# Turning x and the result by block transposes on VectorE and 128-byte DMA pieces, in place of transposes on TensorE

## The chip, the cores and the metric

The kernel runs on one core of a Trainium2 chip (trn2). The metric is device time in microseconds for one launch; three runs were timed. One further execution was profiled. The core has five engines that matter here: TensorE (PE, with its weight loads shown as PEld), VectorE (DVE), ScalarE (ACT), GpSimd (POOL) and SyncE (SP). DMAs are issued by the queues of SP and ACT ("SPq" and "ACTq" in the profile).

## The reference

An attention with RMS-normalised q and k is followed by an MLP mixer. Sizes: batch B = 8, 12 heads of 64, 448 tokens, so 768 channels; the token MLP has 256 hidden units, the channel MLP 1536. All inputs are float32 but the four mixer weights, which are float64.

```python
q_n, k_n = rmsnorm(q, g_q), rmsnorm(k, g_k)
attn = softmax(q_n @ k_n.T / 8)                       # per batch and head
x = (attn @ v).transpose(0, 2, 1, 3).reshape(8, 448, 768)
h = np.maximum(x.transpose(0, 2, 1) @ w_tok1, 0) @ w_tok2   # over tokens
u = x + h.transpose(0, 2, 1)
h2 = np.maximum(u @ w_ch1, 0) @ w_ch2                 # over channels
return u + h2
```

## The kernel before

The work of one batch lives in a tile `uT` of [128 channels, 6 groups of channels, 448 tokens]. Attention writes x into it, transposed: each pair of heads gives one group `j` (the normalisation by the row sums, `denominator`, is the last step and ends on VectorE at L468). So everything has channels on partitions, except for two places:

- the token MLP's first product, `tok1` (L598), needs x with tokens on partitions. `trans_x` makes it, one group of channels at a time, into the tile `x` of [112, 4, 384], one for each half of the channels;
- the result must be written to DRAM with tokens as rows. `trans_y` does that, one group at a time, through a tile `y`.

Both call `turn`: four transposes on TensorE (L577) from `uT` into a PSUM tile of the pool that the attention's scores also use (`ps_S`, 4 buffers), and a copy from PSUM on ACT (L581) or on DVE (L583). `trans_y` then issues one DMA on ACT's queue (L822). There are 48 turns of x and 48 of the result.

The 448 tokens are taken as 112 partitions by 4: partition p holds tokens 4p to 4p + 3, in q's load (`load_qk`, L1006), in the load of `w_tok1` and `w_tok2` (`weight_chunks`), in `x` and in the output DMA. So inside the kernel the tokens are permuted, and put right by the output DMA.

The order of the work on PE, DVE, ACT and POOL is written out by hand; the queue of SP is ordered by the program builder. Work is put into lists of items (a cost in us and a function), and `merge` interleaves the lists evenly by cost. While batch b goes through the mixer, batch b + 1 goes through the attention. One pass of the loop over b does this:

1. `tok1` on half 0 of x, merged with the last two turns of the result of b - 1 (`left`);
2. the attention of the next batch merged with `tok1` on half 1, `tok2` (L606, whose result DVE adds to `uT` at L611), the first channel product `ch1` (L728) and the two-column part of the second, `ch2` (L785);
3. `last_items`: the seven one-column products of `ch2`, in which four turns of this batch's result and six turns of the next batch's x are interleaved.

`tok1` and the products of `ch1`, `ch2` and `tok2` use a PSUM pool `ps_M` of two buffers. The result of `tok1` passes through a ReLU on ACT (L601) into `h1`. The weights of the channel MLP come as "units" through six SBUF buffers by DMAs on SP's queue (L654, `load_units`), five units ahead of their use. In the first batches SP also carries the load, conversion and storage of the weights and of their sums.

```python
l = turns(b, [0, 1, KC, KC + 1])
if b + 1 < B:
    l += x_items(b + 1, 0) + x_items(b + 1, 1)
return [single[0]] + merge(single[1:-1], l) + [single[-1]]
```

The program holds two arms of the whole kernel, chosen by a test on g_q and g_k at run time; the inputs take the first one (`shifted` is False), and all of the profile is of that.

Of the kernel before, what the change touches and what calls it, by code (L numbers as in the profile page):

```python
# [8 lines left out]
F32 = mybir.dt.float32  # L9
# [7 lines left out]
DRAM = bass.MemoryType.DRAM  # L17
# [9 lines left out]
def merge(*lists):  # L27

    totals = [sum(c for c, _ in l) or 1.0 for l in lists]
    done = [0.0] * len(lists)  # L30
    at = [0] * len(lists)
    res = []
    while True:
        live = [i for i in range(len(lists)) if at[i] < len(lists[i])]
        if not live:
            return res
        i = min(live, key=lambda i: (done[i] + lists[i][at[i]][0] / 2) / totals[i])
        c, fn = lists[i][at[i]]
        at[i] += 1
        done[i] += c  # L40
        res.append((c, fn))
# [3 lines left out]
def whole(ctx, tc, shifted, pre, q, k, v, g_q, g_k, moe_w_tok1, moe_w_tok2, moe_w_ch1, moe_w_ch2, out):  # L45


    nc = tc.nc
# [3 lines left out]
    B, H, S, D = q.shape  # L52
# [3 lines left out]
    P = 128  # L56
    NS = 4
    R = S // NS
# [3 lines left out]
    NC = C // P  # L62
    NF = DC // P
    HC = C // 2
    HN = NS // 2
    HS = S // 2
    KC, KF = NC // 2, NF // 2
# [8 lines left out]
    pool = lambda name, bufs, **kw: ctx.enter_context(tc.tile_pool(name=name, bufs=bufs, **kw))  # L76
# [8 lines left out]
    rd_pool = pool("rd_pool", 2)  # L85
    uT_pool = pool("uT_pool", 2)
    x_pool = pool("x_pool", 2)
    y_pool = pool("y_pool", 3)
    h1_pool = pool("h1_pool", 2)
    tu_pool = pool("tu_pool", 1)  # L90
    r_pool = pool("r_pool", 1)
    stage_pool = pool("stage_pool", 3)
    unit_pool = pool("unit_pool", UNITS)
    dram = pool("dram", 1, space=DRAM)
    ps_S = pool("ps_S", 4, space=PSUM)
    ps_O = pool("ps_O", 2, space=PSUM)
    ps_M = pool("ps_M", 2, space=PSUM)

    ident, one_c, expo_c, g_t = pre.ident, pre.one_c, pre.expo_c, pre.g_t
    w1_sb = const.tile([P, NS, DT], F32, name="w1_sb")  # L100
    w2_sb = const.tile([P, NJ, NS, R], F32, name="w2_sb")
# [12 lines left out]
    WCOLS = 512  # L114

    def weight_chunks():

        first, second = [], []
        w1v = moe_w_tok1.rearrange("(p c) n -> p c n", c=NS)
        for c in range(0, NS, 2):  # L120
            first.append((R, [w1v[:, c:c + 2, :].rearrange("p c n -> p (c n)")], w1_sb[0:R, c:c + 2, :].rearrange("p c n -> p (c n)"), None))
        for j in range(NJ):
            dst = w2_sb[:, j].rearrange("p c r -> p r c")
            first.append((P, [moe_w_tok2[j * P:(j + 1) * P, :]], dst, NS))

        for w, group, m, t in stages:
            rows = (DC if w is moe_w_ch2 else C) // 2
            src = [w[r:r + P].rearrange("p (i n) -> p i n", i=2)[:, :, m * P:(m + 1) * P]
                   for r in (t * P, rows + t * P)]
            second.append((P, src, None, None))  # L130
        return first, second

    def stage_list():
# [4 lines left out]
        return l  # L138

    def columns(i):  # L140
        return WCOLS if chunks[i][2] is None else chunks[i][1][0].shape[-1]

    def raw_tile():
        return raw_pool.tile([P, WCOLS, 2], U32, name="raw")

    def weight_load(i):
        rows, srcs, dst, split = chunks[i]
        n = columns(i) // len(srcs)
        wide = srcs[0].dtype == I64
        t = raw_tile()  # L150
        if not wide:
            t = t[:].rearrange("p n w -> p (n w)").bitcast(F32)
        for k, src in enumerate(srcs):
            to = t[0:rows, k * n:(k + 1) * n]
            if wide:
                src = src.bitcast(U32)
                to = to.rearrange("p (i n) w -> p i (n w)", i=2) if dst is None else to.rearrange("p n w -> p (n w)")
            elif dst is None:
                to = to.rearrange("p (i n) -> p i n", i=2)
            nc.sync.dma_start(out=to, in_=src)  # L160
        st["raw", i] = t

# [68 lines left out]
            out=hi, in0=hi, scalar=0x80000000, in1=e, op0=ALU.bitwise_and, op1=ALU.bitwise_or)  # L231

    def convert_last(i):
        rows, srcs, dst, split = chunks[i]
        n = columns(i)
        if dst is None:
            q = st["stage", i - len(first)] = stage_pool.tile([P, 4, P], F32, name="stage")
            dst = q[:].rearrange("p q n -> p (q n)")
        fold = (lambda a: a.rearrange("p (r c) -> p r c", c=split)) if split else (lambda a: a)
        t = st.pop(("raw", i))  # L240
        if srcs[0].dtype != I64:
            nc.gpsimd.tensor_copy(out=dst, in_=fold(t[0:rows, 0:n]))
        else:
            lo, hi = (fold(t[0:rows, 0:n, w].bitcast(F32)) for w in range(2))
            nc.gpsimd.tensor_tensor(out=dst, in0=lo, in1=hi, op=ALU.mult)  # L245
    def weight_items(lo, hi):

# [322 lines left out]

    def turn(b, j, dst, by_act):

        ps = s_tile("t_ps")
        for c in range(NS):
            nc.tensor.transpose(  # L577
                ps[0:R, c * P:(c + 1) * P], st["uT", b][:, j, c * R:(c + 1) * R], ident[:, :])
        src = ps[0:R, :].rearrange("p (c n) -> p c n", c=NS)
        if by_act:  # L580
            nc.scalar.copy(out=dst, in_=src)  # L581
        else:
            nc.vector.tensor_copy(out=dst, in_=src)  # L583

    def trans_x(b, j):

        half, o = divmod(j * P, HC)
        if o == 0:
            st["x", half] = x_pool.tile([P, NS, HC], F32, name="x")
        turn(b, j, st["x", half][0:R, :, o:o + P], j % 2)  # L590

    def tok1(b, jc, h):
        cs = slice(h * HC, (h + 1) * HC)
# [223 lines left out]
            into(nc.vector, 1, 0, got)  # L817

    def trans_y(b, cc):
        y = y_pool.tile([P, NS, P], F32, name="y")  # L820
        turn(b, cc, y[0:R], True)
        nc.scalar.dma_start(  # L822
            out=out[b].rearrange("(p c) n -> p c n", c=NS)[:, :, cc * P:(cc + 1) * P], in_=y[0:R])

    turns = lambda b, cs: [(0.5, lambda cc=cc: trans_y(b, cc)) for cc in cs]
    us = lambda n, cols: n * cols * 4 / 2400

    def x_items(b, h):
        return [(0.5, lambda j=j: trans_x(b, j)) for j in range(h * NC // 2, (h + 1) * NC // 2)]

    def tok1_items(b, h):
        return [(us(NS, HC), lambda j=j, h=h: tok1(b, j, h)) for j in range(NJ)]
# [16 lines left out]
    def last_items(b, sums):  # L849


        single = [(us(6, HS), lambda i=i: ch2(b, 1, i, 0)) for i in range(7)]
        if b == 0:
            single = merge(
                [(us(6, S), lambda o=o, h=h: ch2_first(o, h, 2)) for o in range(2) for h in range(2)], sums)
        l = turns(b, [0, 1, KC, KC + 1])
        if b + 1 < B:
            l += x_items(b + 1, 0) + x_items(b + 1, 1)
        return [single[0]] + merge(single[1:-1], l) + [single[-1]]


# [36 lines left out]
    per = NPAIR * 2  # L898
    att_items = lambda lo, hi: [it for g in range(lo, hi) for it in att_step(g)]
# [5 lines left out]
    for b in range(B):  # L905
        early, double = middle_items(b)
        if b == 0:
            begin = x_items(0, 1) + tok1_items(0, 0) + tok1_items(0, 1)
            early = merge(begin + early, weight_items(BEFORE, then)) + merge(
                double, weight_items(then, len(chunks) + 3) + sums[:6])  # L910
        else:

            for _, fn in merge(tok1_items(b, 0), left):
                fn()
            if b == 1:
                early, double = merge(early, sums[12:33]), merge(double, sums[33:])
            early = tok1_items(b, 1) + early + double
        lo = (b + AHEAD) * per + 1
        att = att_items(lo, lo + per) if b + AHEAD < B else []
        for _, fn in merge(att, early) + last_items(b, sums[6:12]):  # L920
            fn()
        left = turns(b, [2, KC + 2])
# [4 lines left out]
class Start:  # L927
# [66 lines left out]
    def load_qk(self, p, st, other=None):  # L994


        b, hs = self.heads(p)
        D, NS, P = self.D, self.NS, 128
        if ("qk", p) not in st:
            st["qk", p] = self.qk_t[p % 3]  # L1000
        qk = st["qk", p]
        nk = (NS - 1) * P
        q = qk[0:self.R, 0:2 * NS * D].rearrange("p (c h d) -> p c h d", c=NS, h=2)
        k = qk[:, 2 * NS * D:4 * NS * D - 2 * D].rearrange("p (c h d) -> p c h d", c=NS - 1, h=2)
        for a in range(2):
            self.nc.sync.dma_start(out=q[:, :, a], in_=self.q[b, hs][a].rearrange("(p c) d -> p c d", c=NS))  # L1006
        for a in range(2):
            (other or self.nc.sync).dma_start(
                out=k[:, :, a], in_=self.k[b, hs][a][0:nk].rearrange("(p c) d -> p c d", c=NS - 1))
        for a in range(2):  # L1010
            o = 4 * NS * D - 2 * D + a * D
            self.nc.sync.dma_start(out=qk[a * D:(a + 1) * D, o:o + D], in_=self.k[b, hs][a][nk:])
# [124 lines left out]
```

## Time and profile before

| | |
|---|---|
| median of 3 runs | 1450.26 us (1448.8 to 1451.36) |
| the profiled execution | 1450.25 us; span of its instructions 1448.5 us |
| PE busy | 97% of the span |
| DVE, ACT, POOL busy | 47%, 33%, 29% |
| clock granted to TensorE | 0.989 of full speed |
| mean DMA rate | 152 GB/s, 256811 packets, 108004 of them under 512 bytes |
| PE transposes of L577 | 384 |

The busy shares are averages over the span. A row of the profile names the line of the kernel, the engine, the operation and "out<-in" by the tiles' names; where an engine sat idle, the row ends with the idle time and with what ended it, after an arrow. A DMA has two times: how long its issue held the queue, and how long after the start of the issue its data had landed. A product in float32 appears as two matmul records, so that 6 matmuls are "x12".

### The profile page before, as it was taken

The numbers are of one execution on the slowest core, as the hardware profiler recorded it, in microseconds if no ns is written. First come the engines' busy times: TensorE is split into PE (matmuls) and PEld (weight loads), VectorE is DVE, ScalarE is ACT, GpSimd is POOL, SyncE is SP. The second block draws the span as 40 slices with busy tenths as digits, with TensorE's granted clock in tenths as the row PEclk, the third lists the DMA queues.
The fourth block names the chain that finished last, engine by engine and source line by source line (L and its number), as shares of the span: only waits on it lengthen the run. The fifth ranks groups of instructions, "written<-read, shape, count | busy, mean of one in ns | idle before, by whom it ended". The sixth has DMA issues, their size and how long they took to land.

```text
span 1448.5 us, 19051 instructions
## 1 busy us (share of the span) xinstructions
PE 1398.2 (97%) x6832; PEld 992.3 (69%) x6832; DVE 681.5 (47%) x1270; ACT 471.5 (33%) x845; POOL 423.3 (29%) x425
## 2 busy tenths in 40 slices
PE   5888989999999999999999999999999999999998
PEld 2333434456778677785787767785877847777997
DVE  7878887316543444425543255334454244332311
ACT  5644445223332233223332233323332233212111
POOL 1122323417763123312332033321233123311230
PEclk9988999999999999999999999999999999999999
DMA  6556768565986245452545434452454514334453
GB/s 175 167 154 196 217 184 237 158 188 162 269 255 209 76 128 149 137 167 65 154 128 150 132 101 144 142 172 69 135 145 144 161 46 142 124 114 132 142 174 117
DMA packets 256811, 219.47 MB, mean 152 GB/s; under 512 B 108004, under 2 KB 215524, under 8 KB 256708
## 3 DMA queue, kind: packets, MB, share of 16 engines
q1 hardware_dynamic: 233506, 206.96, 48.3%
q10 hardware_dynamic: 23074, 11.21, 3.0%
q8 instruction: 56, 0.92, 0.3%
q14 instruction: 47, 0.39, 0.1%
q0 software_dynamic: 128, 0.00, 0.0%
HBM read 188.22 MB, written 29.88 MB: 151 GB/s over the span
## 4 chain that ended last, share of the span: by engine, by line
PE 88%; DVE 6%; issue 2%; SPq 1%; DMA 1%; ACT 1%; POOL 0%; ACTq 0%; DVEq 0%; POOLq 0%
PE m_ps L728 24%; PE m_ps L785 23%; PE s_ps L320 8%; PE o_ps L421 8%; PE m_ps L598 5%; PE m_ps L606 4%; PE m_ps L709 4%; PE m_ps L691 3%; PE t_ps L577 3%; PE t_ps L300 2%; PE d_ps L400 2%; PE o_ps L433 1%; PE s_ps L334 1%; DVE raw L211 1%; DVE raw L230 1%
## 5 line engine op out<-in xcount | busy, mean ns | idle before, releaser
L785 PE MATMUL m_ps<-hb,unit 128*128 128x224 f32 x1764 | 349.7, 354 | 0.1
L785 PEld LDWEIGHTS m_ps<-hb,unit 128*128 128x128 f32 x1764 | 327.8, 190 | 17.0 <-issue 12.1
L310 ACT ACTIVATE e<-s_ps,rs 128x448 f32<-128x448 f32 x336 | 187.4, 634 | 209.0 <-PE s_ps L320 133.8
L728 PE MATMUL m_ps<-tu,unit 128*128 128x224 f32 x1008 | 204.5, 354 | 0.0
L728 PEld LDWEIGHTS m_ps<-tu,unit 128*128 128x128 f32 x1008 | 187.5, 190 | 9.2 <-PE o_ps L421 4.2
L728 PE MATMUL m_ps<-uT,unit 128*128 128x224 f32 x756 | 153.8, 356 | 1.8 <-DVE uT L611 1.8
L728 PEld LDWEIGHTS m_ps<-uT,unit 128*128 128x128 f32 x756 | 141.0, 190 | 19.8 <-issue 16.4
L320 PE MATMUL s_ps<-qkT 64*128 64x448 f32 x576 | 142.5, 589 | 5.3 <-ACT qkT L302 2.8
L421 PE MATMUL o_ps<-e,v 128*64 128x448 f32 x576 | 133.2, 566 | 0.0
L794 POOL TENSOR_TENSOR uT<-uT,r 128x448 f32<-128x448 f32 (+1 forms) x56 | 50.0, 903 | 224.7 <-DVE r L794 144.0
L381 POOL TENSOR_TENSOR es<-e 128x896 f32<-128x896 f32 x42 | 89.8, 2138 | 71.0 <-ACT sq L1029 51.4
L290 POOL TENSOR_TENSOR qk_t<-qk_t,rs 112x512 f32<-112x512 f32 x36 | 39.3, 1113 | 239.9 <-DVE rs L1067 200.6
L320 PEld LDWEIGHTS s_ps<-qkT 64*128 64x128 f32 x576 | 51.5, 192 | 72.4 <-issue 55.8
L462 DVE STREAM_TRANSPOSE dt<-d_ps 128x448 f32<-128x448 f32 x42 | 27.3, 650 | 153.2 <-PE d_ps L400 153.1
L302 ACT ACTIVATE qkT<-t_ps,g_t 128x448 f32<-128x448 f32 (+1 forms) x96 | 60.3, 660 | 118.8 <-PE t_ps L300 117.6
L421 PEld LDWEIGHTS o_ps<-e,v 128*64 128x64 f32 x576 | 33.2, 137 | 86.8 <-issue 82.3
L794 DVE TENSOR_TENSOR uT<-uT,m_ps 128x448 f32<-128x448 f32 (+1 forms) x70 | 34.1, 502 | 117.3 <-PE m_ps L785 117.1
L733 DVE TENSOR_TENSOR r<-m_ps,r 128x448 f32<-128x448 f32 x63 | 39.2, 622 | 106.3 <-POOL r L733 63.2
L606 PE MATMUL m_ps<-w_sb,h 128*128 128x448 f32 x192 | 80.8, 564 | 8.6 <-DVE uT L611 8.5
L598 PE MATMUL m_ps<-x,w_sb 112*128 112x384 f32 x256 | 88.1, 489 | 0.0
L387 DVE TENSOR_TENSOR es<-es,e 128x896 f32<-128x896 f32 x42 | 46.3, 1103 | 87.8 <-ACT e L310 63.8
L245 POOL TENSOR_TENSOR stage<-raw 128x512 f32<-128x512 f32 x36 | 41.5, 1154 | 143.5 <-DVE raw L230 66.4
(93 smaller groups left out, 1584.5 us busy)
## 6 DMA issues: line engine op xcount, KB each, us to landing
unit<-ws SPq DMA_DIRECT2D x318, 384.0 KB, 3.3
raw<-in_moe_w_ch_dram SPq DMA_DIRECT2D x72, 256.0 KB, 3.4
out_dram<-y ACTq DMA_DIRECT2D x48, 224.0 KB, 3.3
qk_t<-in_q_dram SPq DMA_DIRECT2D x84, 112.0 KB, 3.5
v<-in_v_dram SPq DMA_DIRECT2D x48, 192.0 KB, 2.7
ws<-stage SPq DMA_DIRECT2D x36, 256.0 KB, 3.8
raw<-ws SPq DMA_DIRECT2D x36, 256.0 KB, 3.8
ws<-raw SPq DMA_DIRECT2D x36, 256.0 KB, 3.6
```

The source lines that it names most:

```text
L302: nc.scalar.mul(to, ps[:, 0:NS * n], g_t[:, i:i + 1])
L310: nc.scalar.activation(out=out, in_=ps[:, 0:S], func=AF.Exp, scale=st["rs", p][:, r:r + 1])
L320: nc.tensor.matmul(out=pss[a][:, 0:S], lhsT=qkT[a * D:(a + 1) * D, o:o + P], rhs=qkT[a * D:(a + 1) * D, 0:S], start=True, stop=True)
L381: nc.gpsimd.tensor_tensor(out=es[:], in0=st["e", p, 0][:], in1=st["e", p, 1][:], op=ALU.add)
L387: nc.vector.tensor_tensor(out=es[:], in0=es[:], in1=st["e", p, 2][:], op=ALU.add)
L421: nc.tensor.matmul(out=o[a * D:(a + 1) * D, 0:S], lhsT=vt[:, c:c + D], rhs=e[:, a, :], start=start, stop=stop)
L598: nc.tensor.matmul(out=ps[:, 0:HC], lhsT=w1_sb[0:R, c, jc * P:(jc + 1) * P], rhs=st["x", h][0:R, c, :], start=(c == 0), stop=(c == NS - 1))
L606: nc.tensor.matmul(out=ps[:, 0:S], lhsT=st["h1", jc][:, cc * P:(cc + 1) * P], rhs=w2_sb[:, jc].rearrange("p c r -> p (c r)"), start=(jc == ...
L709: nc.tensor.matmul(out=ps[:, 0:S], lhsT=w, rhs=natural(half)[:, :, t, :], start=(half == 0 and t == 0), stop=(half == 1 and t == KF - 1))
L728: nc.tensor.matmul(out=ps[:, j * HS:(j + 1) * HS], lhsT=w[:, t, j, :], rhs=m, start=(t == 0), stop=(t == KC - 1))
L785: nc.tensor.matmul(out=ps[:, j * HS:(j + 1) * HS], lhsT=st["w"](j, t), rhs=hb[:, HB[what], t, :], start=(t == 0), stop=(t == KF - 1))
L794: add = lambda e, o, x, y: e.tensor_tensor(out=o, in0=x, in1=y, op=ALU.add)
```

## The change

`turn` no longer uses TensorE, PSUM or a copy. VectorE transposes the 32x32 blocks of one group of `uT` (128 channels by 448 tokens) in one instruction, from SBUF to SBUF, into a tile of a new pool with four buffers. Four DMAs, one for each block row of 32 channels, then put the pieces at their places in DRAM: 32 x 14 pieces of 32 floats (128 bytes) each. For the result they go straight to the output, issued by ACT. For x they go into a DRAM tile `xs` of [448, 384], issued by SP, and when three groups are done one DMA on SP reads the half of x back into `x` with tokens on partitions.

The tokens are in natural order: token c x 112 + p lies on partition p, chunk c. So the loads of q and of `w_tok1` have another pattern, and `w_tok2` is taken without a fold of its columns.

The order changes too: half 0 of the next batch's x is turned in the middle of the attention, after its eighth step, and half 1 at the head of the list in `last_items`, ahead of the result's turns. The cost of a turn in the lists is 0.1 in place of 0.5.

```diff
-    y_pool = pool("y_pool", 3)
+    turn_pool = pool("turn_pool", 4)
...
+    xs_pool = pool("xs_pool", 2, space=DRAM)
...
-        w1v = moe_w_tok1.rearrange("(p c) n -> p c n", c=NS)
+        w1v = moe_w_tok1.rearrange("(c p) n -> p c n", c=NS)
...
-            dst = w2_sb[:, j].rearrange("p c r -> p r c")
-            first.append((P, [moe_w_tok2[j * P:(j + 1) * P, :]], dst, NS))
+            first.append((P, [moe_w_tok2[j * P:(j + 1) * P, :]], w2_sb[:, j].rearrange("p c r -> p (c r)")))
...
-    def turn(b, j, dst, by_act):
-
-        ps = s_tile("t_ps")
-        for c in range(NS):
-            nc.tensor.transpose(
-                ps[0:R, c * P:(c + 1) * P], st["uT", b][:, j, c * R:(c + 1) * R], ident[:, :])
-        src = ps[0:R, :].rearrange("p (c n) -> p c n", c=NS)
-        if by_act:
-            nc.scalar.copy(out=dst, in_=src)
-        else:
-            nc.vector.tensor_copy(out=dst, in_=src)
+    def turn(b, j, engine, dst):
+
+
+        t = turn_pool.tile([P, S], F32, name="turned")
+        nc.vector.transpose(out=t[:], in_=st["uT", b][:, j, :])
+        for i in range(0, P, 32):
+            engine.dma_start(
+                out=dst[:, i:i + 32].rearrange("(n t) c -> t n c", t=32),
+                in_=t[i:i + 32].rearrange("t (n c) -> t n c", c=32))
 
     def trans_x(b, j):
 
         half, o = divmod(j * P, HC)
         if o == 0:
-            st["x", half] = x_pool.tile([P, NS, HC], F32, name="x")
-        turn(b, j, st["x", half][0:R, :, o:o + P], j % 2)
+            st["xs", half] = xs_pool.tile([S, HC], F32, name="xs")
+        xs = st["xs", half]
+        turn(b, j, nc.sync, xs[:, o:o + P])
+        if o + P == HC:
+            st["x", half] = x = x_pool.tile([P, NS, HC], F32, name="x")
+            nc.sync.dma_start(out=x[0:R], in_=xs[:].rearrange("(c p) n -> p c n", c=NS))
+            st.pop(("xs", half))
...
     def trans_y(b, cc):
-        y = y_pool.tile([P, NS, P], F32, name="y")
-        turn(b, cc, y[0:R], True)
-        nc.scalar.dma_start(
-            out=out[b].rearrange("(p c) n -> p c n", c=NS)[:, :, cc * P:(cc + 1) * P], in_=y[0:R])
-
-    turns = lambda b, cs: [(0.5, lambda cc=cc: trans_y(b, cc)) for cc in cs]
+        turn(b, cc, nc.scalar, out[b][:, cc * P:(cc + 1) * P])
+
+    turns = lambda b, cs: [(0.1, lambda cc=cc: trans_y(b, cc)) for cc in cs]
...
-        return [(0.5, lambda j=j: trans_x(b, j)) for j in range(h * NC // 2, (h + 1) * NC // 2)]
+        return [(0.1, lambda j=j: trans_x(b, j)) for j in range(h * NC // 2, (h + 1) * NC // 2)]
...
-        l = turns(b, [0, 1, KC, KC + 1])
-        if b + 1 < B:
-            l += x_items(b + 1, 0) + x_items(b + 1, 1)
+        l = x_items(b + 1, 1) if b + 1 < B else []
+        l += turns(b, [0, 1, KC, KC + 1])
...
-        att = att_items(lo, lo + per) if b + AHEAD < B else []
+        att = []
+        if b + AHEAD < B:
+            att = att_items(lo, lo + 8) + x_items(b + AHEAD, 0) + att_items(lo + 8, lo + per)
...
-            self.nc.sync.dma_start(out=q[:, :, a], in_=self.q[b, hs][a].rearrange("(p c) d -> p c d", c=NS))
+            self.nc.sync.dma_start(out=q[:, :, a], in_=self.q[b, hs][a].rearrange("(c p) d -> p c d", c=NS))
```

In the changed file the transpose stands at L578, its DMAs at L580, the read of x at L593, `tok1` at L602 with its ReLU at L605, and `tok2` at L610.

More of the change, by code (lines that the diff above doesn't have):

```diff
@@ L118, in weight_chunks @@
         first, second = [], []
-        w1v = moe_w_tok1.rearrange("(p c) n -> p c n", c=NS)
+        w1v = moe_w_tok1.rearrange("(c p) n -> p c n", c=NS)
         for c in range(0, NS, 2):
-            first.append((R, [w1v[:, c:c + 2, :].rearrange("p c n -> p (c n)")], w1_sb[0:R, c:c + 2, :].rearrange("p c n -> p (c n)"), None))
+            first.append((R, [w1v[:, c:c + 2, :]], w1_sb[0:R, c:c + 2, :].rearrange("p c n -> p (c n)")))
         for j in range(NJ):
-            dst = w2_sb[:, j].rearrange("p c r -> p r c")
-            first.append((P, [moe_w_tok2[j * P:(j + 1) * P, :]], dst, NS))
+            first.append((P, [moe_w_tok2[j * P:(j + 1) * P, :]], w2_sb[:, j].rearrange("p c r -> p (c r)")))
         for w, group, m, t in stages:
@@ L129, in weight_chunks @@
                    for r in (t * P, rows + t * P)]
-            second.append((P, src, None, None))
+            second.append((P, src, None))
         return first, second
@@ L140, in columns @@
     def columns(i):
-        return WCOLS if chunks[i][2] is None else chunks[i][1][0].shape[-1]
+        src = chunks[i][1][0]
+        return WCOLS if chunks[i][2] is None or len(src.shape) == 3 else src.shape[-1]
     def raw_tile():
@@ L146, in weight_load @@
     def weight_load(i):
-        rows, srcs, dst, split = chunks[i]
-        n = columns(i) // len(srcs)
+        rows, srcs, dst = chunks[i]
         wide = srcs[0].dtype == I64
         t = raw_tile()
+        flat = t[0:rows].rearrange("p n w -> p (n w)")
         if not wide:
             t = t[:].rearrange("p n w -> p (n w)").bitcast(F32)
+            flat = t[0:rows]
+        n = columns(i) // len(srcs) * (1 + wide)
         for k, src in enumerate(srcs):
-            to = t[0:rows, k * n:(k + 1) * n]
+            to = flat[:, k * n:(k + 1) * n]
             if wide:
                 src = src.bitcast(U32)
-                to = to.rearrange("p (i n) w -> p i (n w)", i=2) if dst is None else to.rearrange("p n w -> p (n w)")
-            elif dst is None:
-                to = to.rearrange("p (i n) -> p i n", i=2)
+            if len(src.shape) == 3:
+                to = to.rearrange("p (i n) -> p i n", i=src.shape[1])
             nc.sync.dma_start(out=to, in_=src)
@@ L233, in convert_last @@
     def convert_last(i):
-        rows, srcs, dst, split = chunks[i]
+        rows, srcs, dst = chunks[i]
         n = columns(i)
@@ L238, in convert_last @@
             dst = q[:].rearrange("p q n -> p (q n)")
-        fold = (lambda a: a.rearrange("p (r c) -> p r c", c=split)) if split else (lambda a: a)
         t = st.pop(("raw", i))
         if srcs[0].dtype != I64:
-            nc.gpsimd.tensor_copy(out=dst, in_=fold(t[0:rows, 0:n]))
+            nc.gpsimd.tensor_copy(out=dst, in_=t[0:rows, 0:n])
         else:
-            lo, hi = (fold(t[0:rows, 0:n, w].bitcast(F32)) for w in range(2))
+            lo, hi = (t[0:rows, 0:n, w].bitcast(F32) for w in range(2))
             nc.gpsimd.tensor_tensor(out=dst, in0=lo, in1=hi, op=ALU.mult)
```

## The prediction

> **What bounds the kernel now.** I read the page's busy table and the chain that ended last first, to learn which engine carries the time.
>
> ```profile
> PE 1398.2 (97%) x6832; PEld 992.3 (69%) x6832; DVE 681.5 (47%) x1270; ACT 471.5 (33%) x845; POOL 423.3 (29%) x425
> ...
> PE 88%; DVE 6%; issue 2%; SPq 1%; DMA 1%; ACT 1%; POOL 0%; ACTq 0%; DVEq 0%; POOLq 0%
> ```
>
> TensorE is the bound: whatever PE no longer does is worth its own time, as long as nothing makes PE wait. The second view is the weight-load timeline around the end of a batch, where L577 (the transposes to be removed) lies.
>
> ```profile
> 642.24 2.19 PEld L785 LDWEIGHTS m_ps<-hb,unit 128*128 128x128 f32 x12
> 644.44 0.54 PEld L577 LDWEIGHTS t_ps<-ident,uT 128*112 128x112 f32 x4
> 644.95 2.19 PEld L785 LDWEIGHTS m_ps<-hb,unit 128*128 128x128 f32 x12
> 647.15 2.32 PEld L598 LDWEIGHTS m_ps<-x,w_sb 112*128 112x128 f32 x8
> ...
> 658.66 2.23 PEld L598 LDWEIGHTS m_ps<-x,w_sb 112*128 112x128 f32 x8 [0.70 <-ACT e L310]
> ...
> 661.63 0.30 PEld L606 LDWEIGHTS m_ps<-w_sb,h 128*128 128x128 f32 x2
> ```
>
> One turn (four transposes) takes 644.95 - 644.44 = 0.5 us of PE with no gap on either side; 96 turns are 48 us. The seven single-column products begin about 626.95 (the first transpose, 629.14, less 2.19), so the boundary up to the first tok2 (L606) takes 661.63 - 626.95 = 34.7 us. Third, the prices of the pieces: the tile view of y, the source views of L1006 and L462, and the page's DMA queues.
>
> ```profile
> L822 ACTq DMA_DIRECT2D out_dram<-y x48: 578/579/712, 287.4 to 1443.0; - x48
> DMA to landing us min/median/max: 2.9/3.3/7.9
> ```
>
> ```profile
> L1006 SPq DMA_DIRECT2D qk_t<-in_q_dram x84: 596/612/1454, 39.8 to 1198.7; - x84
> DMA to landing us min/median/max: 2.5/3.5/6.6
> ```
>
> ```profile
> L462 DVE STREAM_TRANSPOSE dt<-d_ps x42: 649/650/652, 142.5 to 1298.3; 128x448 f32<-128x448 f32 x42
> ```
>
> ```profile
> q1 hardware_dynamic: 233506, 206.96, 48.3%
> q10 hardware_dynamic: 23074, 11.21, 3.0%
> ```
>
> A DMA of 448 pieces holds its queue 0.6 us and lands 3 to 4 us after its issue. A block transpose is 0.65 us. From the two queue rows: 47.9 ns for a packet of 886 bytes, 30.1 ns for 486, so about 8.5 ns + 0.0445 ns a byte: 14 ns for 128 bytes.
>
> **What the Trainium skill says.** "DMA: Bandwidth & Descriptors", Specifications: under 512 bytes a transfer misses line rate, as the DMA engine reads, modifies and writes. No write to DRAM in this trace is under 512 bytes, so nothing here confirms or denies it; it is the upper bound below. The same page, "Two DMAs through the same engine are not ordered": a DMA that reads what another wrote must wait for its completion semaphore; so the read of x waits for a landing. "Issuing engines are not separate DMA queues": SP and ACT share the 16 engines, a second queue saving only issue time. "VectorE: DVE Perf Modes", The three transpose paths: DVE transposes 32x32 blocks only; hence the four DMAs that place the blocks.
>
> **The change part by part.** Removed from PE: 96 x 0.5 = 48 us. Removed from DVE and ACT: 24 copies of 0.69 and 72 of 0.59 us. Added to DVE: 96 x 0.65 = 62 us. On SP: 48 turns x 4 = 192 issues plus 16 reads, 208 x 0.61 = 127 us, in a queue whose issues now fill about a third of the span. On ACT: 192 issues for 48, net 144 x 0.58 = 84 us, less 42 us of copies. DMA engines: 96 x 1792 packets x 14 ns / 16 = 153 us, reads of x 16 x 448 x 77 / 16 = 34, less y's 48 x 448 x 31 / 16 = 42: plus 145 us, from 51% to about 61%. None of these totals binds; their place does. The loads of q and w_tok1 keep their packet count or nearly (q pieces are 256 bytes in SBUF either way); moving w_tok2 without a fold changes two Pool copies; I set these at nothing, under the weight pipeline of the first 100 us, or under 1 us if uncovered.
>
> *A boundary (seven).* In the built program all SP and ACT DMAs draw on eight completion semaphores in turn, and each waits until the one eight places before has landed; the turned tile has four buffers. Time from the first single product, without turns on PE: products end at 2.2, 4.4 ... 15.4; tok1 half 0 takes 15.4 to 20.8 (2 x 2.7). DVE turns x after the evictions of products 1 and 2 (its order), at 2, 5.7 and 7.9; y at 10, 10.7, 12.7, 14.5, then two after 16. With 0.63 us per issue and a landing of 4.0 us: x pieces are issued 2.5-5, 5.7-8.4 and, each waiting for its eighth predecessor, 9.7-12.4. ACT issues y turn 0 at 10.1-12.5; y turn 1 waits for turn 0 to land (14.1-16.5). A unit load queued on SP ahead of the read of x shares a semaphore with turn 1 and waits to 18.1; the read waits to 18.7 and lands at 23. y turn 2 ends 20.5. y turn 3's second DMA waits for the read to land (23); its last issue ends 24.8. Only then does ACT do the ReLU of tok1 half 0 (ready since 18.1): 25.3. PE needs that PSUM buffer for tok1 half 1: due 20.8, starts 25.3. Two more turns of issues on ACT (to 27.7 and 30.6) sit before the next ReLUs; tok2 starts at 34.0. So 6 us saved (12 turns), 5.3 lost: -0.7 x 7 = -5 us. Repeated with landing 3.2, tok2 starts at 32.0, so about 2.5 us of boundary per us of landing. The first boundary has the weight-sum DMAs on SP, the last no attention work to put between: +3 each, +6. Behind the blocked SP stand five units loaded ahead, about 10 us of bare products and twice that with attention between: no stall. Losing that cover would cost about 3 us, one landing, per boundary.
>
> *The start.* Batch 0's second half of x has no lead: its last turns come when DVE frees, about 110.7 (x<-t_ps ran at 110.05). Twelve issues with their waits take to 118.5, landing 122, read lands 126; PE wants it at 113.45 (second half of L598). +12.6.
>
> *Mid-batch.* x half 0 moves into the attention: three transposes stand together on DVE (2 us) ahead of PSUM evictions that have two buffers of 2.2 us: 0 to 2 us, I take 1, seven times: +7. Its SP block (12 issues, a landing, a read, some 12 us) is covered by the five units.
>
> *The end.* Last product to end of program now 8.3 us (1440.2 to 1448.5); after: eviction 0.75, two transposes 1.3, eight issues 5, a landing 3, about 10.3; four turns before it save 2. Zero.
>
> Unknown: how long a 128-byte write to DRAM takes. Below: the 512-byte ones' 2.9 us landing[...]. Above: 28 ns a packet in place of 14, an estimate that counts the skill's read-modify-write as two passes. A gain over the 256-byte loads' 2.5 us is not excluded. I take 4.0, as the burst is denser than any of before.
>
> Sum: -5 + 6 + 12.6 + 7 + 0 = **+20.6 us**. The profiled execution took 1450.25 us (span 1448.5 and 1.75 around it), the median of the runs is 1450.26, so 1470.
>
> **The rivals.**
> Faster: landings stay below the break-even. If the start, the two odd boundaries and the DVE clusters cost 26 us together, seven boundaries must gain 3.7 each: a landing of 2.8; if only the start costs, 3.5. For it: y's DMAs in quiet stretches land in 2.9. Against: they land alone there, and 36 DMAs would now share eight semaphores. At 2.9: 7 x (34.7 - 31.2) = -24, +10, about 1436. Chance 0.17.
> Slower by far: the 128-byte writes cost double, and the boundary is bound by DMA. 36 us hold 16.6 us of DMA now (share 0.46); less y's 5.2, plus 36 x 448 x 28 / 16 = 28 and the read 2: 42 us where PE needs 34. 7 x 7.3 = 51, start 20, clusters 10: about 1531. Chance 0.2.
> No change: saving and waits balance to within 3 us. Chance 0.06.
> The change not doing what it says: PE still transposing uT; the queue order shows none left, so no chance is put on it.
>
> **How the numbers follow.** The boundary wait, 0.57, gives 1470 (own range 1453 to 1492). A measurement of this kernel tells about 0.2% (2.9 us) from no change. Faster 0.17, same 0.06, slower 0.77. The range reaches to the faster rival and most of the way to the DMA-bound one: 1436 to 1520.
>
> **What would show it.** PE's L577 gone and PE's share of the span down from 97 to about 93%; PE idle before tok1 (L602) or tok2 (L610), ended by ACT h (L605) or by the DMA into x (L593); the largest single wait near 113 us, some 12 us long; ACT's L580 issues back to back with landings near 4 us; DMA share about 60%. Wrong: PE without waits at the boundaries (then it is faster), PE waiting for units (then the lookahead was too short), or landings far over 5 us with the DMA share near 1 there (then the pieces were mispriced).

## The result, and the profile after

The changed kernel takes 1474.83 us (median of 4 runs, 1473.84 to 1479.86); the kernel before took 1450.81 us beside it (4 runs). The ratio is 1.0173, with a 95% interval of 1.0147 to 1.0200: slower by 24 us. The prediction said 1470.

These are the lines of the page after that answer to those of before: the busy table, the chain that ended last, and the two DMA queues (packets, MB, share of the 16 engines' time).

```profile
PE 1368.7 (93%) x6448; PEld 959.8 (65%) x6448; DVE 717.0 (49%) x1342; ACT 428.7 (29%) x773; POOL 422.3 (29%) x425
...
q1 hardware_dynamic: 330242, 228.99, 55.9%
q10 hardware_dynamic: 89890, 11.22, 4.9%
...
PE 76%; DMA 8%; DVE 5%; issue 1%; SPq 1%; ACT 1%; ACTq 1%; POOL 1%; DVEq 0%; POOLq 0%
```

PE lost its 384 transposes and is busy 29.5 us less, yet the span is 24.4 us longer. The transposes alone were some 48 us; but the 256 matmul records of `tok1`'s products, the same before and after, are busy 20.1 us longer (busy us and mean ns, then the idle time ahead):

```profile
L598 PE MATMUL m_ps<-x,w_sb 112*128 112x384 f32 x256 | 88.1, 489 | 0.0
L602 PE MATMUL m_ps<-x,w_sb 112*128 112x384 f32 x256 | 108.2, 580 | 57.3 <-ACT h L605 42.6
```

PE's share of the chain falls from 88 to 76%, and DMA, at 1% before, now has 8%. So PE waits for something that a transfer releases. Which instructions wait is seen in the list of waits (total, times, longest, in us), here of PE alone:

```profile
PE m_ps L602 <- ACT h L605: 42.6, 7, 6.9
PE m_ps L602 <- DMA x<-xs: 14.7, 2, 7.7
```

There is one wait for each of the seven boundaries, about 6.1 us long, for the ReLU on ACT (L605) that has to free a PSUM buffer; and there are two at the start, where batch 0's x itself is late. The timeline of the boundary that was shown of before (start, duration, engine, line; in brackets the idle time ahead and what ended it):

```profile
643.38 16.80 ACTq L580 DMA_DIRECT2D out_dram<-turned  x16
648.82 4.90 PEld L602 LDWEIGHTS m_ps<-x,w_sb 112*128 112x128 f32 x16
...
650.01 0.32 SPq L593 DMA_DIRECT2D x<-xs  x1
...
660.23 0.49 ACT L605 ACTIVATE h<-m_ps 128x384 f32<-128x384 f32 x1 [24.29 <-DMA out_dram<-turned]
660.31 2.15 ACTq L580 DMA_DIRECT2D out_dram<-turned  x4
...
660.77 5.49 PE L602 MATMUL m_ps<-x,w_sb 112*128 112x384 f32 x8 [6.43 <-ACT h L605]
...
669.23 2.85 PE L602 MATMUL m_ps<-x,w_sb 112*128 112x384 f32 x8
...
672.20 0.30 PEld L610 LDWEIGHTS m_ps<-w_sb,h 128*128 128x128 f32 x2
```

Half 0 of `tok1` is done at about 654. Its first ReLU starts at 660.23, directly after ACT's sixteenth piece DMA, and PE goes on at 660.77. Sixteen issues of 0.49 us are 8 us; they took 16.8. The trace records which completion semaphore each DMA draws on, and every update of it. The DMAs of SP and ACT share eight semaphores, and an issue stands until the DMA that drew on its semaphore before has landed. ACT stood four times in this row, 8.2 us in all:

| ACT's DMA came out at | after standing, us | the last DMA on its semaphore | which landed at |
|---|---|---|---|
| 649.09 | 1.6 | a piece of ACT, issued 645.00 | 649.07 |
| 652.79 | 1.0 | a weight unit of SP, issued 649.41 | 652.72 |
| 655.61 | 2.2 | the read of x, issued 650.01 | 655.58 |
| 659.33 | 3.4 | a piece of ACT, issued 650.53 | 659.30 |

It is the same in all five boundaries out of batches 1 to 5: ACT stands 1.8 to 3.2 us until the read has landed, and then 1.0 to 3.4 us for a piece that was 7.4 to 8.8 us in flight beside it. In the last boundary it stands for pieces alone, up to 8.5 us in flight. The second thing to see is the pace: the eight matmul records after the wait take 5.49 us, eight like them at 669.23 take 2.85. Such stretches are the 20.1 us of above.

Why did pieces of 56 KB land so late? The page's DMA issues (KB each, median us to landing) and the same list for the window from 649 to 656 us:

```profile
xs<-turned SPq DMA_DIRECT2D x192, 56.0 KB, 2.0
x<-xs SPq DMA_DIRECT2D x16, 672.0 KB, 6.8
out_dram<-turned ACTq DMA_DIRECT2D x192, 56.0 KB, 2.8
```

```profile
unit<-ws SPq DMA_DIRECT2D x4, 384.0 KB, 5.8
x<-xs SPq DMA_DIRECT2D x1, 672.0 KB, 5.6
out_dram<-turned ACTq DMA_DIRECT2D x7, 56.0 KB, 6.0
```

A piece lands in 2.0 to 2.8 us as a rule, but in 6.0 beside the read and four units. The table by stretches (columns: stretch, its length, busy time of PE, PEld, DVE, ACT, POOL, PE's clock, DMA share, GB/s) says the same:

```profile
649.00:656.00 7.00, 5.33 (x17) 2.86 (x16) 2.11 (x4) 0.00 (x0) 0.00 (x0) 1.00 0.89 252
656.00:661.00 5.00, 0.23 (x1) 0.23 (x2) 0.00 (x0) 0.49 (x1) 0.00 (x0) 0.59 0.99 272
```

For 12 us the transfer engines are 89 and 99% busy, and at the end of this PE's clock has dropped. The changed kernel has such a half-clock record at each of the seven boundaries (at 312, 486, 657, 831, 1002, 1172 and 1346 us); the kernel before has none there.

The account by stages, read from PE's instructions in the two traces. A boundary runs from the first single-column product of `ch2` to the first `tok2`; the first one, out of batch 0, lies in the second row.

| us | before | after | difference |
|---|---|---|---|
| start to the first `tok2` | 121.7 | 134.5 | +12.8 |
| first `tok2` to the second (batch 0, first boundary) | 200.6 | 190.0 | -10.6 |
| batch 1, `tok2` to the single products | 136.0 | 137.3 | +1.3 |
| the same in batches 2 to 5, each | 133.8 | 133.8 | 0 |
| six boundaries, sum | 205.1 | 225.9 | +20.8 |
| last single products to the end | 25.9 | 26.1 | +0.2 |

What the table leaves out is equal in both (135.3 us in batch 6, 88.6 in batch 7). The differences add up to 24.5 us, and the spans differ by 24.4.

### The profile page after: what moved, and what is told of

Same layout as the page of the kernel before. It is cut to its first block, busy times and chain, and to the rows that moved or that the text cites. A ratio compares the mean times of both kernels' runs of the same rounds, so it can differ in the third digit from the quotient of the medians.

```text
span 1472.9 us, 18833 instructions
## 1 busy us (share of the span) xinstructions
PE 1368.7 (93%) x6448; PEld 959.8 (65%) x6448; DVE 717.0 (49%) x1342; ACT 428.7 (29%) x773; POOL 422.3 (29%) x425
## 3 DMA queue, kind: packets, MB, share of 16 engines
q10 hardware_dynamic: 89890, 11.22, 4.9%
## 4 chain that ended last, share of the span: by engine, by line
PE 76%; DMA 8%; DVE 5%; issue 1%; SPq 1%; ACT 1%; ACTq 1%; POOL 1%; DVEq 0%; POOLq 0%
PE m_ps L732 23%; PE m_ps L789 19%; PE s_ps L321 7%; PE o_ps L422 7%; DMA out_dram<-turned 5%; PE m_ps L602 5%; PE m_ps L610 4%; PE m_ps L695 3%; PE t_ps L301 2%; PE d_ps L401 2%; PE m_ps L713 1%; PE o_ps L434 1%; PE s_ps L335 1%; DMA xs<-turned 1%; DMA unit<-ws 1%
## 5 line engine op out<-in xcount | busy, mean ns | idle before, releaser
L789 PE MATMUL m_ps<-hb,unit 128*128 128x224 f32 x1764 | 343.1, 354 | 1.1 <-DMA unit<-ws 1.0
L789 PEld LDWEIGHTS m_ps<-hb,unit 128*128 128x128 f32 x1764 | 330.8, 190 | 18.4 <-issue 12.7
L311 ACT ACTIVATE e<-s_ps,rs 128x448 f32<-128x448 f32 x336 | 187.0, 634 | 201.5 <-PE s_ps L321 127.3
L602 PE MATMUL m_ps<-x,w_sb 112*128 112x384 f32 x256 | 108.2, 580 | 57.3 <-ACT h L605 42.6
L321 PE MATMUL s_ps<-qkT 64*128 64x448 f32 x576 | 140.7, 589 | 5.5 <-ACT e L311 2.8
L602 PEld LDWEIGHTS m_ps<-x,w_sb 112*128 112x128 f32 x256 | 56.7, 228 | 104.9 <-ACT h L605 46.9
L605 ACT ACTIVATE h<-m_ps 128x384 f32<-128x384 f32 x32 | 15.7, 491 | 250.2 <-DMA out_dram<-turned 170.9
L610 PE MATMUL m_ps<-w_sb,h 128*128 128x448 f32 x192 | 77.3, 545 | 5.1 <-DVE uT L615 5.0
```

What stands on the lines that cost most here:

```text
L311: nc.scalar.activation(out=out, in_=ps[:, 0:S], func=AF.Exp, scale=st["rs", p][:, r:r + 1])
L321: nc.tensor.matmul(out=pss[a][:, 0:S], lhsT=qkT[a * D:(a + 1) * D, o:o + P], rhs=qkT[a * D:(a + 1) * D, 0:S], start=True, stop=True)
L602: nc.tensor.matmul(out=ps[:, 0:HC], lhsT=w1_sb[0:R, c, jc * P:(jc + 1) * P], rhs=st["x", h][0:R, c, :], start=(c == 0), stop=(c == NS - 1))
L610: nc.tensor.matmul(out=ps[:, 0:S], lhsT=st["h1", jc][:, cc * P:(cc + 1) * P], rhs=w2_sb[:, jc].rearrange("p c r -> p (c r)"), start=(jc == ...
L789: nc.tensor.matmul(out=ps[:, j * HS:(j + 1) * HS], lhsT=st["w"](j, t), rhs=hb[:, HB[what], t, :], start=(t == 0), stop=(t == KF - 1))
```

## The experiments

The theory, A: ACT's piece DMAs are held back, because each waits for the landing of the DMA that used its semaphore before it, the read of x among them; the ReLU stands behind them in ACT's order, and PE behind the ReLU. The rivals: ACT's issue time alone is enough (R); transfers or x come late whoever does what (D); natural order costs (O). A clock that drops while PE waits (K) may add to A. All ratios are against the kernel before, run on the same chip.

**y_on_sp: the result's pieces issued by SP.**

```diff
-        turn(b, cc, nc.scalar, out[b][:, cc * P:(cc + 1) * P])
+        turn(b, cc, nc.sync, out[b][:, cc * P:(cc + 1) * P])
```

> The changed kernel with the result's 192 piece DMAs issued by SP in place of ACT; all else stays. Theory A (the boundary is lost on ACT: its queue of piece DMAs is held by the eight shared semaphores behind the read of x, and the ReLU of tok1 stands behind it): tok1 no longer waits for ACT, PE's wait before L602 falls from about 115 us in all to under 30, six boundaries fall from about 37.7 to 30 to 32 us, and the kernel takes about 1430 us. Theory B (the read of x comes too late, whoever issues the result): PE waits for the DMA into x in place of ACT, boundaries stay at 36 us or more, about 1470 us. Theory C (DMA engines saturated by small pieces): as B, with landings unchanged, 1465 to 1480 us.

Measured: 1431.13 us, ratio 0.9872 (0.9855 to 0.9888). One word turns a loss of 24 us into a gain of 19. (The 115 us of the expectation add the idle time of PE and that of its weight loads; PE's own wait for the ReLU, 42.6 us, falls to 3.5.) PE's wait, and the timeline of the same boundary in this kernel:

```profile
PE m_ps L602 <- ACT h L605: 3.5, 6, 0.6
```

```profile
642.02 6.25 SPq L580 DMA_DIRECT2D out_dram<-turned  x7
644.57 2.32 PEld L602 LDWEIGHTS m_ps<-x,w_sb 112*128 112x128 f32 x8
...
647.54 0.49 ACT L605 ACTIVATE h<-m_ps 128x384 f32<-128x384 f32 x1 [15.86 <-PE m_ps L602]
648.08 4.81 PEld L602 LDWEIGHTS m_ps<-x,w_sb 112*128 112x128 f32 x16 [1.20 <-ACT h L605]
...
659.02 0.30 PEld L610 LDWEIGHTS m_ps<-w_sb,h 128*128 128x128 f32 x2
```

The ReLU now waits for its own product and for nothing else. PE's wait for it, 0.6 us, stands between the two products of half 0, and half 1 follows them without a gap. The boundaries are 30.3 us (five) and 26.9, in sum 178.6 against 225.9.

The transfers are no quicker from issue to landing: pieces of the result land in 3.2 us, the read in 6.4. But the read starts sooner. In the changed kernel SP is held by ACT's pieces too: the unit load ahead of the read, at 649.41, came out as a piece of ACT landed, at 649.34. In the last six boundaries the read is issued 11.6 to 13.0 us after the boundary's first product here, and 13.8 to 17.7 us after it in the changed kernel. So this run takes away two things, the hold on ACT and the late start of the read; the next one parts them. Batch 1, though, takes 147.4 us against 136.0; of that below.

**relu_dve: the ReLU moved to VectorE, all transfers where they are.**

```diff
-        nc.scalar.activation(out=st["h1", jc][:, cs], in_=ps[:, 0:HC], func=AF.Relu)
+        nc.vector.tensor_scalar(out=st["h1", jc][:, cs], in0=ps[:, 0:HC], scalar1=0.0, scalar2=None, op0=ALU.max)
```

> The changed kernel with the ReLU of the third layer on VectorE in place of ScalarE; all transfers and their queues stay. Theory A (what costs is that the ReLU stands in ScalarE's queue behind the issues of the result's pieces): the boundaries fall from 37 to 39 us to about the 30.3 us of y_on_sp, the total to 1432 to 1440; ScalarE's issues are as late as before and nobody waits for them. Rival D (in the changed kernel the 12 us from 649 to 661 us have the transfer engines at 89 to 99% busy, so that x's half 1 or the weight units come late whoever does the ReLU): boundaries of 35 us or more, 1460 or above.

Measured: 1439.29 us, ratio 0.9909 (0.9888 to 0.9929); boundaries 31.2, 30.9, 33.6, 30.8, 31.0 and 26.1, in sum 183.6. This decides against D: with the crowd of transfers left as it was (the read is issued 13.8 to 17.1 us after the boundary's first product, ACT's pieces stay), the boundary is short once the ReLU has left ACT's order. PE's waits before `tok1` end on the read or on DVE, and none on ACT; the 7.9 and 7.0 us are those of the start:

```profile
PE m_ps L602 <- DMA x<-xs: 15.4, 5, 7.9
PE m_ps L602 <- DVE nt L1068: 7.0, 1, 7.0
PE m_ps L602 <- DVE turned L578: 2.4, 2, 1.3
```

In the six boundaries after the first they are 0 to 2.2 us, where the changed kernel has 5.3 to 6.4. So much and no more is left to the late read and to the order of DVE. ACT's list of waits has the hold in a new place: the attention's exponentials (L311), where it cost less.

```profile
ACT e L311 <- DMA out_dram<-turned: 115.2, 4, 29.6
```

It is not free: the stretches after the boundaries take up to 2.9 us more than 133.8 (136.7, 135.2, 133.8 and 135.0 in batches 2 to 5), and batch 1 takes 142.4 in place of 137.3.

**x_pe and x_pe_spread: x by TensorE, so no pieces and no read of x; the result by pieces on ACT as in the changed kernel.** The two differ only in the cost that `merge` sees.

```diff
-        turn(b, j, nc.sync, xs[:, o:o + P])
+        turn_pe(b, j, st["x", half][0:R, :, o:o + P], j % 2)   # x_pe: cost 0.5; x_pe_spread: cost 0.1
```

> The changed kernel with x turned by TensorE and copied as before (no DMA tile xs, no read of x); the result still goes by block transposes and 192 piece DMAs on ACT. PE gets 48 x 0.5 = 24 us back. Theory A (the ACT queue is held by the semaphores that the read of x and the units behind it share): without the read the ReLUs wait little, about 1430 us. Rival R (24 issues of 0.5 us per boundary on ACT are enough to hold the ReLU): ACT's wait for piece DMAs before L605 stays over 100 us in all, boundaries near 37 us, about 1460 us.

Measured for x_pe: 1470.92 us, ratio 1.0145 (1.0126 to 1.0164): the number of rival R. But the edit had moved something else. With x's items at 0.5 and the result's at 0.1, the turns of the result were put behind x's, at the end of the single products:

```profile
657.90 10.61 ACTq L580 DMA_DIRECT2D out_dram<-turned  x16
...
668.56 0.49 ACT L612 ACTIVATE h<-m_ps 128x384 f32<-128x384 f32 x1 [14.04 <-DMA out_dram<-turned]
```

Sixteen issues in one row, 0.66 us each and never more than 0.3 us apart, begin 2.5 us before `tok1` does at 660.36 and outlast it. So the run shows that issue time alone can do the harm if it stands in the wrong place, and not that it did so in the changed kernel, where the row began 5.4 us before `tok1` (643.38 and 648.82). The same kernel with equal costs tells:

> x turned by TensorE as in x_pe, the result by pieces issued by ScalarE, but with the changed kernel's cost of 0.1 for both kinds of item, so that the four turns of the result are spread over the single products as in the changed kernel, and not pushed behind x's at their end. Theory A (ScalarE is held because its pieces share the completion semaphores with the read of x): with no read of x there is nothing that holds them; the boundaries come back to about the 32 us that y_pe had, 210 - 190 = 20 us less than x_pe: about 1450 or less. Rival R (ScalarE's own issue time, 0.66 us a piece, is enough to hold the ReLU wherever the pieces stand): 1465 to 1472, as x_pe.

Measured: 1444.69 us, ratio 0.9961 (0.9946 to 0.9976); boundaries 32.3 to 34.5 and 29.0, in sum 193.2. Without the pieces and the read of x on SP, the result's pieces in their old place cost little: theory A. R keeps a small part, as PE still waits for the ReLU 12.9 us in seven waits, against 42.6, and 4.5 of them in the first boundary:

```profile
PE m_ps L609 <- ACT h L612: 12.9, 7, 4.5
```

What no run separates is the two ways in which the read holds ACT: through the shared semaphore itself, or by crowding the engines so that pieces land late and hold their successors. The trace of the changed kernel has both: in the five boundaries out of batches 1 to 5, ACT stood 11.5 us for the read itself and 13.2 us for the pieces in flight beside it.

**y_pe: the result by TensorE and one DMA, x by pieces.**

```diff
-        turn(b, cc, nc.scalar, out[b][:, cc * P:(cc + 1) * P])
+        turn_pe(b, cc, y[0:R], True)
+        nc.scalar.dma_start(out=out[b].rearrange("(c p) n -> p c n", c=NS)[:, :, cc * P:(cc + 1) * P], in_=y[0:R])
```

> The changed kernel with the result turned by TensorE, copied by ACT and sent by one DMA as before; x still goes by block transposes, pieces through DRAM and the read. To fit in SBUF the turned tile has 2 buffers in place of 4 and y has 2 in place of 3. PE gets 24 us back. Theory A (what is lost at the boundaries needs the result's pieces on ACT): no wait of tok1 on ACT, about 1430 us. Theory B (the read of x is late by itself): tok1 waits for the DMA into x by 4 us or more at each boundary, 1455 us or more. In both, the first wait for x near 115 us stays, about 13 us.

Measured: 1458.31 us, ratio 1.0077 (1.0047 to 1.0107), its four runs spread from 1455.67 to 1465.57. So theory A was right on the boundaries and its 1430 wrong. Its boundaries are clean, 32.1 (five) and 29.7, and PE has no wait for the ReLU. It loses in the first batches: the second `tok2` comes at 331.2 (322.3 before) and batch 1 takes 147.2. To make room the edit had also cut the turned tile from four buffers to two, and DVE waits 63.3 us in all for them; how much of the loss is due to that was not tried.

**keep_clock and keep_clock2: spare products on PE while it would wait.**

```diff
+            st["b"] = b
+            keep_busy(14)    # keep_clock2: 7; products of 448 columns that nobody reads
```

> The changed kernel with 14 spare products (448 columns, 0.38 us each, 5.3 us) put on TensorE between tok1 on half 0 and tok1 on half 1 of batches 1 to 7; their result is not used. In the changed kernel the weight loads of the tok1 that follows the wait come at 0.64 us a pair in place of 0.33 and the record of the granted clock shows a half there. Theory K (the idle time itself halves the clock, so a wait of 6.5 us costs another 2.7 us): with PE busy during the wait tok1 runs at full pace at once, 7 x 2.7 = 19 us less, about 1456 us. Rival (the half pace is from something else, or the spare products delay the path): no gain or up to 37 us slower, 1475 to 1510 us.

Measured: 1493.62 us, ratio 1.0294 (1.0272 to 1.0317). The size was wrong: one product is two records of 0.38 us, so the 14 took 10.6 us in place of 5.3, more than the wait. What the run still shows: the eight records after them took 2.74 us, and no boundary has a half-clock record.

> The changed kernel with 7 spare 448-column fp32 products (14 matmul records of 0.38 us, about 5.3 us) on TensorE between the third layer's half 0 and half 1 at each of the seven boundaries, half of what keep_clock had; they compute nothing that is used. In the changed kernel TensorE stands there for 6.4 to 7 us, so that they should fit in the wait. Theory K (a TensorE that stood idle comes back at half its clock, 5.4 instead of 2.7 us for the eight records that follow): 7 x 2.7 = 19 us less than the changed kernel's 1475, about 1456, with no half-clock record at the boundaries. Rival N (the late start is all there is; whatever follows is late by the wait, the pace of the eight records is hidden by the next wait): 1475, within 3 us.

Measured: 1466.22 us, ratio 1.0106 (1.0088 to 1.0124). PE's timeline of the boundary:

```profile
651.36 5.33 PE L602 MATMUL m_ps<-x,w_sb 112*128 112x384 f32 x16
656.52 5.42 PE L836 MATMUL idle_ps<-uT,w_sb 112*128 112x448 f32 x14
662.59 2.85 PE L602 MATMUL m_ps<-x,w_sb 112*128 112x384 f32 x8 [0.64 <-ACT h L605]
```

PE is kept from its next product about as long, but at work, and the eight records are back at 2.85 us. From the start of half 1 to `tok2` five of the boundaries take 8.4 us each, against 10.7 in the mean in the changed kernel. The six boundaries sum to 211.8, 14.1 us less than in the changed kernel, where 6 x 2.7 = 16 were expected. Batch 1 took 3.4 us of this back (140.7 against 137.3) and batch 6 1.6 (136.8 against 135.3), and batch 0 with the first boundary gave nothing (190.4 against 190.0), so that the total fell by 9 of the 19. K is shown for its place, and is worth some 2.4 us of a boundary.

**both_pe: both turned by TensorE, the rest of the change kept** (natural order, and half 0 of x in the attention).

> Both x and the result turned by TensorE as before, with what else the change has: tokens in natural order in every load and store, and x's half 0 turned in the middle of the attention part. It tells whether the order alone costs anything. Theory A: nothing, 1450 within 3 us, the boundaries 34 to 35 us. Rival O (natural order makes q's and the weights' loads or the result's store slower, or the earlier half 0 takes a gap that the attention needed): 1456 or more.

Measured: 1448.86 us, ratio 0.9990 (0.9981 to 0.9999). The order costs nothing. The boundaries are 33.5 us (five), a little under the 34 to 35 expected, as half 0's turns have left them for the attention, whose stretches take 135.1 in place of 133.8.

**mixed and mixed2: y_on_sp with a few turns of x given back to TensorE.** Two places are left in y_on_sp. At the start, the read of batch 0's half 1 has no lead. In batch 1, PE waits 7.5 us for weight units, in three waits between 370 and 450 us, where SP also carries the weight sums; the unit loads issued just behind the read of x at 416.06 took 7 to 9 us to land. A half-clock record of 10.2 us, from 417.8 on, goes with them.

```diff
+        if (b, half) in ((0, 1), (2, 0)):     # mixed2: and (0, 0)
+            if o == 0:
+                st["x", half] = x_pool.tile([P, NS, HC], F32, name="x")
+            turn_pe(b, j, st["x", half][0:R, :, o:o + P], j % 2)
+            return
```

> y_on_sp (the result's pieces issued by SP) with six of the 48 turns of x given back to TensorE: half 1 of batch 0, which the start waits for, and half 0 of batch 2, which stands in batch 1 where the weight sums' transfers are. Six turns cost 6 x 0.5 = 3 us. Theory S (batch 1 of y_on_sp is 11 us longer than before because the 672 KB read of x, 7.0 us from issue to landing, stands between the weight units' loads there; and the first token product is 12.3 us late because of batch 0's half 1): batch 1 falls to 136 to 138 us, the first token product to 122 to 124 us, of which some 10 us were given back within batch 0 already: 1431 + 3 - 11 - 2, about 1419 to 1423. Rival T (batch 1 is long because 94 us of work stood still earlier and its weight sums are late anyway): batch 1 stays at 145 to 147, the total at 1430 to 1433.

Measured: 1419.71 us, ratio 0.9785 (0.9754 to 0.9816). Batch 1 fell from 147.4 to 137.2. It is 137.2 in mixed2 too, whatever the start, so this goes to the pieces and the read of x that no longer stand between the unit loads. The first `tok2` came at 129.5 only, not at 122 to 124: half 0 of batch 0 has no lead either, once half 1 is quick.

> mixed with half 0 of batch 0 turned by TensorE too (three more turns, 1.5 us): in mixed the first product of the third layer still waits 8.5 us for the read of that half, and comes back at half clock (5.5 instead of 2.8 us). If that wait were all, the first token product would come at 129.5 + 1.5 - 8.5 - 2.7 = about 120 us. As with mixed, batch 0 may give much of it back (there 4.5 us earlier at the start left 1.9 at the next batch): 1420 - 4 to 1420 - 9, 1411 to 1416; if batch 0's end is set by something else, 1420.

Measured: 1413.51 us, ratio 0.9738 (0.9717 to 0.9759). The first `tok2` comes at 121.0, the second at 307.7 (mixed: 315.2). This is the fastest kernel of the study, 37.6 us below the kernel before. All of PE's waits in the third layer's first product that remain, and its chain:

```profile
PEld m_ps L619 <- ACT h L622: 7.2, 6, 1.2
PE m_ps L619 <- ACT h L622: 3.5, 6, 0.6
```

```profile
PE 81%; DVE 3%; ACT 1%; issue 0%; DMA 0%; SPq 0%; DVEq 0%; ACTq 0%
```

## Why the prediction was right, and where its terms were off

The number, 1470 against 1474.83, and the sign were right, and so was the mechanism: ACT's pieces held behind the read of x, the ReLU behind them, PE behind the ReLU. relu_dve and x_pe_spread each take away one link, and y_on_sp the hold on ACT together with the read's late start; each brings the boundary back. But that the sum of +20.6 came so near is luck. Against its terms, the six boundaries were 22 us worse (+20.8 in place of -1.2), the start with batch 0 and the first boundary 12.7 us better (+2.2 in place of +14.9), and mid-batch 5.7 us better.

- **The turns on PE**, 48 us: right. PE is busy 29.5 us less though `tok1` takes 20.1 more, which makes 49.6. In y_on_sp, with little left to wait for, a boundary is 4.5 us shorter than before (30.3 against 34.8).
- **The boundaries**, -0.7 each: measured +3.5 each (20.8 / 6). Two steps of the working are behind this, given here for the first five of the six. First, half 1 of `tok1` was to start 25.3 us after the first single product; it started at 26.7 to 27.8, mean 27.4. The read is not what was off: 23 was said for its landing, and it landed at 22.6 to 23.9, issued sooner and longer in flight (5.6 to 6.2 us, where 4.3 was said). But the piece that held ACT after it was 7.4 to 8.8 us in flight, where 4.0 was assumed for all. Second, the step from there to `tok2` was taken as 8.7 us, PE at its full pace; it took 9.9 to 11.4, mean 10.7. The two means make 38.1 in place of 34.0. The first step was mis-sized, the second missing: what a wait does to the pace after it. The Trainium skill has it, in "TensorE: Matmul & The Clock Gate", Part 1, The HAM clock gate: after an idle window of about 3.4 us TensorE runs at half its clock. The trace agrees for the boundary shown, with a wait of 6.43 us and then 5.49 in place of 2.85 us. But shorter waits were enough here, as the last section tells. y_on_sp and keep_clock2, where PE doesn't stand, spend 8.6 and 8.4 us on the second step.
- **First and last boundary**, +3 each: the last went from 31.3 to 35.2 us, +3.9 where -0.7 + 3 was said. The first can't be parted from batch 0; its reason was right, as ACT stood 4.2 us there for a transfer of the weight sums.
- **The start**, +12.6: measured +12.8, and mixed2 takes it away. The size was right by luck. One wait of 12.6 us was said, for half 1 of x; there were two, 7.7 us for half 0 and 7.0 for half 1, and after each of them eight records took 4.8 and 4.6 us in place of 2.75. Batch 0 doesn't keep all of it, either: the next row of the table is 10.6 us shorter. Part of that is the turns that PE no longer does there. The other part is seen where the start alone differs: mixed2 has its first `tok2` 13.0 us earlier than y_on_sp and its second only 9.4 earlier.
- **Mid-batch**, +7: nothing. Batches 2 to 5 take 133.8 us in both kernels, so the three transposes that stand together on DVE held no eviction that PE needed. Batch 1's cover of five units did hold in the changed kernel (+1.3), but not in y_on_sp (+11.4).
- **The end**, 0: +0.2.

The rivals: the faster one asked for landings of 2.8 to 3.5 us. The pieces did as well or better in the median, 2.0 and 2.8, but the read and the pieces beside it did not, and it is in that stretch that PE waits. The slower one, a boundary bound by DMA because small writes cost double, has its symptom (0.99 of the engines busy) without its cause. The share of the q10 row gives 0.049 x 16 x 1472.9 / 89890 = 13 ns a packet, against 14 reckoned and 28 feared. "DMA: Bandwidth & Descriptors", Specifications, names a read-modify-write under 512 bytes; no doubling for 128-byte pieces shows here. What fills the engines is large: one read of 672 KB and four units of 384 KB. The lower end of the landings, 2.9 us, was no bound: the pieces' median is below it. The DMA share (61%) came out as written. PE's share did too (93%), but not for its reason: 1398.2 less 48, over a span of 1469, is 92%, and the 20 us of slower records made up the rest. The longest wait of PE was 7.7 us, not 12.

## What to carry to other kernels

Look at what stands behind a DMA issue on its engine before choosing the queue: an issue that must wait for an earlier transfer holds every instruction after it, so that the change lost 24 us with the result's pieces on ScalarE and gained 19 with them on SyncE, which has only other transfers to hold. With eight semaphores for two queues, the transfer waited for may be the other queue's. Add to a wait of TensorE of 2 us or more the half pace that mostly followed it here. And when a turn goes through memory, keep the old way where there is no lead for the round trip: nine turns of 96 left on TensorE were worth 18 us more.

## What the runs showed that had not been expected

- A step of half clock, after short waits too. Over `tok1`'s products in all twelve kernels, eight records took at most 2.85 us after every wait of up to 1.63 us, and 4.1 to 5.5 us after every wait of 1.70 us or more, but for one of 2.41 us, which 2.85 followed. The shortest slow one (x_pe_spread):

```profile
986.05 4.54 PE L609 MATMUL m_ps<-x,w_sb 112*128 112x384 f32 x8 [1.70 <-ACT h L612]
```

- Work that nobody reads, put into the wait, made the kernel faster by 9 us (1474.83 to 1466.22).
- 128-byte pieces to DRAM landed in 2.0 us in the median, sooner than any other transfer in the page's list of issues, and cost 13 ns of an engine each; a 672 KB read took 6.8 us, and pieces in flight beside it up to 8.8.
- A cost in a list of items is a placement. 0.5 in place of 0.1 for x's turns moved the result's turns to the end of the single products, and was worth 26 us (1470.92 against 1444.69).
